# Other priority offsets in the table that breaks ties between operations of a fused attention and mixture-of-experts kernel

## The chip, the cores and the metric

The kernel runs on one core of a Trainium2 chip. Its time is device microseconds of one execution. Five engines work side by side: PE (TensorE, matrix multiplication), DVE (VectorE), ACT (ScalarE), POOL (GpSimd) and SP (SyncE, which here only starts transfers). Each takes its own list of instructions strictly in the order in which the list was written; an instruction whose inputs aren't there holds all that stands behind it on its engine.

## The reference

A decaying attention without softmax, of 8 batches and 8 heads with 576 tokens and 64 elements a head, and a layer of 8 experts on its result, of which each token uses two:

```python
scores = scale * np.matmul(q, k.transpose(0, 1, 3, 2))
gamma = 1.0 - 2.0 ** (-5.0 - np.arange(H))
Dmat = np.where(rel >= 0, gamma[:, None, None] ** rel[None, :, :], 0.0)
x = np.matmul(scores * Dmat, v)            # -> (4608, 512)
noisy = x @ w_gate + np.log1p(np.exp(x @ w_noise)) * noise
top2 = np.argpartition(-noisy, 2, axis=1)[:, :2]   # their softmax: top2_w
for e in range(8):
    for k in range(2):
        mask = top2[:, k] == e
        h = np.maximum(x[mask] @ w1[e], 0.0)       # 512 -> 1024
        out[mask] += top2_w[mask, k, None] * (h @ w2[e])
```

## The kernel before

**Attention** comes in 16 units of four heads of one batch; four units make a batch pair. SP loads q, k and v (L663 and L673). They are cast to bf16 and scaled with the decay: k on ACT (L712), q on DVE or POOL (L721), v on DVE or POOL (L728). PE turns k and q (L750, L744), and the copies out of PSUM go to ACT (L459) or DVE (L461). PE makes scores (L775), which DVE multiplies by the mask as it takes them out of PSUM (L783); then states (L808, into a tile `tb`) and outputs (L843, L853), which ACT or DVE copy into `xT`. The 64 last tokens of each batch pair are a tail of their own: casts L878 (ACT), L881 and L884 (DVE or POOL), turns L893, scores L908 and L913.

**The route** of each batch pair follows its tail: logits (L967), a chain of some 40 small DVE instructions (L977 to L1065) that finds the two experts of each token, ranks on PE (L1030, L1032) from a tile `MM` (L1003), a product `ub` on POOL (L1041), and a table: DVE makes two one-hot tiles, `olo` and `oh` (L1074), ACT writes the values `val` into the same PSUM tile (L1063), DVE multiplies (L1076), PE multiplies the two (L1081). From it come the row numbers `xi` (L1095). The rows of x are turned (L1110) and stored to `xd` in DRAM by SP.

**The experts** gather their rows from `xd` (L1246, indirect DMAs that POOL issues, two of them for one tile pair, with a small memset L444 between two that follow one another). What is filled from the first three batch pairs is computed already between the attention units (up L1328, down L1418), the rest afterwards in wide tiles (L1354, L1418, L1437; relu L1337 and L1339; scaling L1471, L1473; scatter L1483).

**What sets the order.** The program is recorded as operations with their inputs and outputs, and a planner writes the five lists out. It goes through the ready operations and takes the one that can start first by its own costs; of those that can start within the same twentieth of a microsecond, the one with the lowest priority:

```python
key = (round(t * 20), o.prio, o.i)
```

An operation that two engines may do goes to the one on which it ends first by the same costs. Every call site has a name, and a table `ORDER` of 149 names with six columns adds an offset to the priority. The column is chosen by how far on the operation lies: four of them for attention, one for the batch pair at its end and one for the wide tiles:

```python
prio += ORDER[at][min(3, int(max(0.0, prio)) // 4) if prio < 60 else 4 if prio < 136 else 5]
```

The choice of one operation moves all that come later, since tiles and PSUM buffers are handed out in the same pass. In the first 170 us of its plan the planner also puts matrix multiplications on PE that nothing reads (L467, the fillers), where it expects PE to wait for data.

Of the kernel before, what the change touches and what calls it, by code (L numbers as in the profile page):

```python
# [38 lines left out]
    "setup1": (-7.25, -7.25, -7.25, -7.25, -7.25, -7.25),  # L39
    "setup2": (5, 5, 5, 5, 5, 5),  # L40
    "setup3": (-4.25, -4.25, -4.25, -4.25, -4.25, -4.25),
    "setup4": (-0.25, -0.25, -0.25, -0.25, -0.25, -0.25),
    "setup5": (-3.25, -3.25, -3.25, -3.25, -3.25, -3.25),
    "setup6": (-1.75, -1.75, -1.75, -1.75, -1.75, -1.75),
    "setup7": (2, 2, 2, 2, 2, 2),
    "setup8": (4, 4, 4, 4, 4, 4),
    "setup9": (-6.5, -6.5, -6.5, -6.5, -6.5, -6.5),
    "setup10": (2, 2, 2, 2, 2, 2),
    "setup11": (2.5, 2.5, 2.5, 2.5, 2.5, 2.5),
    "setup12": (-0.5, -0.5, -0.5, -0.5, -0.5, -0.5),  # L50
    "setup13": (3.5, 3.5, 3.5, 3.5, 3.5, 3.5),
    "setup14": (-6, -6, -6, -6, -6, -6),
    "setup15": (1, 1, 1, 1, 1, 1),
    "setup16": (4.25, 4.25, 4.25, 4.25, 4.25, 4.25),
    "setup17": (-2.5, -2.5, -2.5, -2.5, -2.5, -2.5),
    "setup18": (-1.75, -1.75, -1.75, -1.75, -1.75, -1.75),
    "setup19": (-0.25, -0.25, -0.25, -0.25, -0.25, -0.25),
    "setup20": (-4, -4, -4, -4, -4, -4),
    "setup21": (0.5, 0.5, 0.5, 0.5, 0.5, 0.5),
    "setup22": (1.5, 1.5, 1.5, 1.5, 1.5, 1.5),  # L60
    "setup23": (-0.25, -0.25, -0.25, -0.25, -0.25, -0.25),
    "setup24": (-2.5, -2.5, -2.5, -2.5, -2.5, -2.5),
    "setup25": (-0.5, -0.5, -0.5, -0.5, -0.5, -0.5),
    "setup26": (2.25, 2.25, 2.25, 2.25, 2.25, 2.25),
    "setup27": (1.75, 1.75, 1.75, 1.75, 1.75, 1.75),
    "setup28": (1, 1, 1, 1, 1, 1),
    "setup29": (-3.25, -3.25, -3.25, -3.25, -3.25, -3.25),
    "setup30": (-3.5, -3.5, -3.5, -3.5, -3.5, -3.5),
    "setup31": (-1.5, -1.5, -1.5, -1.5, -1.5, -1.5),
# [12 lines left out]
    "later4": (-1, -1, -1, -1, -1, -1),
    "later5": (0.25, 0.25, 0.25, 0.25, 0.25, 0.25),
    "later6": (5.5, 5.5, 5.5, 5.5, 5.5, 5.5),
    "later7": (7.25, 7.25, 7.25, 7.25, 7.25, 7.25),
    "load1": (1, -1, -2, -3, 1, 1),
    "load2": (-6.75, -4.25, -9.25, -7, -8, -8),
    "load_tail1": (-1.5, -3.5, -1.75, -5.5, -1.5, -1.5),
    "cast1": (0, 0, -0.5, 0, 0, 0),
    "cast2": (-2, 0, 0, 2.5, 0, 0),  # L90
    "cast3": (-1, 1, -5.25, -2, -1, -1),
    "tr1": (-0.5, 2, -1, -1, 0, 0),
    "tr2": (0, 0, 1, 0, 0, 0),
# [1655 lines left out]
```

## Time and profile before

| what | value |
|---|---|
| median of 3 runs | 421.04 us (415.92, 421.04, 424.44) |
| profiled execution | 412.69 us, its span 411.1 us |
| mean granted TensorE clock | 0.989 |
| PE, POOL, ACT, DVE busy | 92%, 71%, 66%, 36% of the span |
| matrix multiplications | 4320, of them 68 fillers |
| moved by DMA | 98.06 MB |

The profile is of one execution, whose time lies below all three timed ones. L numbers are lines of the kernel. The name behind "<-" in brackets is what ended the idle time of an engine; "issue" there means that nothing in the profile did. All times within the span count from its start.

### The profile page before, as it was taken

How to read it: one execution, taken by the hardware profiler on the slowest of the kernel's cores; microseconds unless marked ns; L12 is line 12 of the kernel's file. 1: busy time of each engine (PE TensorE's matmuls, PEld its weight loads, DVE VectorE, ACT ScalarE, POOL GpSimd, SP SyncE). 2: the span in 40 equal slices, each digit the busy share in tenths (PEclk: the TensorE clock that was granted, in tenths of full speed). 3: DMA queues.
4: the chain of work that ended last, by engine and by line, in shares of the span. 5: the costliest groups of instructions: out<-in, count | busy, mean ns of one | idle time of the engine just before them, and what ended most of it. 6: DMA issues, size and time to landing. Idle time of an engine off the chain costs nothing.

```text
span 411.1 us, 11031 instructions
## 1 busy us (share of the span) xinstructions
PE 377.1 (92%) x4320; PEld 233.3 (57%) x4320; DVE 148.2 (36%) x413; ACT 272.3 (66%) x468; POOL 291.0 (71%) x379
## 2 busy tenths in 40 slices
PE   4998867889898898999999999999999999999994
PEld 2567656677575666767556554544554454454453
DVE  8456798788269587220111322101011000000002
ACT  2589978898787765776555877666686445555451
POOL 8676783990799848778676477778675776728564
PEclk9899999989999999999999999999999999999999
DMA  8999998999999989999989899999999998839766
GB/s 226 290 298 255 317 305 254 306 269 252 275 286 205 264 188 284 395 246 221 280 188 377 288 331 223 260 251 230 296 257 211 165 202 152 164 45 133 127 94 131
DMA packets 106184, 98.06 MB, mean 239 GB/s; under 512 B 40975, under 2 KB 83472, under 8 KB 106130
## 3 DMA queue, kind: packets, MB, share of 16 engines
q1 hardware_dynamic: 85858, 60.92, 56.0%
q0 software_dynamic: 17584, 36.24, 43.4%
q8 instruction: 34, 0.56, 0.6%
q10 hardware_dynamic: 2688, 0.18, 0.4%
q14 instruction: 20, 0.16, 0.2%
HBM read 73.11 MB, written 26.10 MB: 241 GB/s over the span
## 4 chain that ended last, share of the span: by engine, by line
PE 65%; DVE 8%; POOL 7%; DMA 6%; issue 6%; ACT 6%; POOLq 0%; SPq 0%; another core or an unknown queue 0%; DVEq 0%; ACTq 0%
PE ps L1418 25%; PE ps L1354 23%; PE ps L1328 6%; POOL out_dram L1483 4%; DMA xd<-xg 2%; ACT half L459 2%; DMA half<-in_v_dram 2%; DVE half L783 2%; PE ps L1437 2%; PE ps L808 2%; PE ps L467 1%; POOL half L721 1%; ACT xT L459 1%; DVE olo L1074 1%; PE ps L1268 1%
## 5 line engine op out<-in xcount | busy, mean ns | idle before, releaser
L1337 ACT ACTIVATE half<-ps 128x512 bf16<-128x512 f32 (+5 forms) x184 | 90.6, 503 | 87.5 <-PE ps L1354 55.0
L1418 PE MATMUL ps<-W,half 128*128 128x512 bf16 x432 | 137.8, 379 | 1.4 <-issue 1.1
L1354 PE MATMUL ps<-big,W 128*128 128x512 bf16 (+4 forms) x448 | 124.5, 326 | 0.6 <-DVE half L1473 0.6
L1246 POOL DMA_INDIRECT xg<-xd,xi x76 | 79.1, 1040 | 48.2 <-DMA half<-in_v_dram 11.7
L1483 POOL DMA_INDIRECT out_dram<-half,xg x71 | 90.3, 1272 | 30.1 <-issue 14.8
L1418 PEld LDWEIGHTS <-half 128*128 128x128 bf16 x568 | 54.5, 98 | 62.8 <-issue 3.1
L1354 PEld LDWEIGHTS <-W 128*128 128x128 bf16 x448 | 43.8, 98 | 33.4 <-issue 0.8
L1354 PE MATMUL ps<-big,xT 128*128 128x512 bf16 (+2 forms) x160 | 47.6, 337 | 0.0
L1471 ACT ACTIVATE half<-ps,xg 128x512 f32<-128x512 f32 (+1 forms) x58 | 39.3, 678 | 10.0 <-PE ps L1418 6.7
L783 DVE TENSOR_TENSOR half<-ps,mask 128x512 bf16<-128x512 f32 x64 | 40.3, 682 | 14.3 <-PE ps L775 10.9
L1418 PE MATMUL ps<-xT,half 128*128 128x512 bf16 x136 | 44.9, 379 | 0.0
L459 ACT ACTIVATE half<-ps 128x1024 bf16<-128x1024 bf16 (+1 forms) x42 | 38.5, 946 | 7.9 <-PE ps L744 4.0
L1473 DVE TENSOR_SCALAR half<-ps,xg 128x512 f32<-128x512 f32 (+1 forms) x17 | 10.6, 623 | 76.8 <-PE ps L1437 42.0
L1328 PE MATMUL ps<-half,W 128*128 128x256 bf16 (+1 forms) x288 | 29.1, 255 | 1.6 <-DVE half L461 0.8
L1339 DVE TENSOR_SCALAR half<-ps 128x512 bf16<-128x512 f32 (+5 forms) x12 | 6.8, 569 | 60.5 <-issue 32.9
L1328 PEld LDWEIGHTS <-W 128*128 128x128 bf16 x288 | 23.7, 98 | 5.8 <-issue 1.8
L467 PE MATMUL ps<-mask,ident__61 128*128 128x512 bf16 x68 | 20.3, 429 | 3.7 <-DVE hpf L527 3.7
L1469 DVE SCALAR_TENSOR_TENSOR half<-ps,xg,half 64x256 f32<-64x256 f32 (+2 forms) x7 | 3.6, 521 | 55.2 <-PE ps L1437 32.4
L1354 PEld LDWEIGHTS <-xT 128*128 128x128 bf16 x160 | 15.6, 98 | 12.8 <-issue 0.4
L459 ACT ACTIVATE tb<-ps 64x512 bf16<-64x512 f32 x32 | 18.9, 591 | 4.0 <-POOL half L721 1.9
L459 ACT ACTIVATE W<-big 128x1024 bf16<-128x1024 f32 x20 | 21.0, 1059 | 0.0
L808 PE MATMUL ps<-half,half 64*64 64x64 bf16 (+2 forms) x512 | 17.2, 213 | 1.7 <-ACT xT L459 1.6
(204 smaller groups left out, 517.0 us busy)
## 6 DMA issues: line engine op xcount, KB each, us to landing
big<-in_moe_w_dram SPq DMA_DIRECT2D x40, 512.0 KB
W<-in_moe_w_dram POOLq DMA_DIRECT2D x12, 512.0 KB
xd<-xg SPq DMA_DIRECT2D x16, 264.0 KB
W<-in_q_dram SPq DMA_DIRECT2D x16, 256.0 KB
big<-in_k_dram SPq DMA_DIRECT2D x8, 512.0 KB
big<-in_v_dram SPq DMA_DIRECT2D x8, 512.0 KB
big<-in_q_dram SPq DMA_DIRECT2D x16, 256.0 KB
W<-in_k_dram SPq DMA_DIRECT2D x6, 512.0 KB
```

Source lines behind the costliest of these rows:

```text
L459: self.nc.scalar.activation(out, in_, Act.Copy)
L467: self.nc.tensor.matmul(b.t, lhsT=ident, rhs=mask.rearrange("p r x -> p (r x)").unsqueeze(1).to_broadcast([P, 2, 2 * P]), start=True, stop ...
L783: nc.vector.tensor_tensor(S.t.bitcast(BF16).rearrange("p (h c x) -> p h c x", h=2, c=2)[:, h], p[h].t.rearrange("p (c x) -> p c x", c=2), ...
L808: nc.tensor.matmul(o[h * HD:(h + 1) * HD, hp, n, :], lhsT=kk[:k, r, c, y], rhs=vv[:k, r, c, y].unsqueeze(1).to_broadcast([k, n.stop - n.st ...
L1246: ins = nc.gpsimd.indirect_dma_start(out=x.t[:n, :], out_offset=None, in_=self.xd[:rows, :], in_offset=IOff(ap=xi.t[:n, h:h + 1], axis=0), ...
L1328: nc.tensor.matmul(pv()[:, f2, :], lhsT=w.t[:, o:o + P], rhs=xv()[:, di, :n], start=(di == 0), stop=(di == KD - 1))
L1337: self.nc.scalar.activation(o, i, Act.Relu)
L1354: self.mm = nc.tensor.matmul(p.t[:, :n], lhsT=w.t[:, o:o + P], rhs=xv()[:, di, :n], start=(di == 0), stop=(di == KD - 1))
L1418: self.mm = self.nc.tensor.matmul(po.t, lhsT=hv[:, c:c + P], rhs=self.W[e].t[:, o:o + DM], start=(f == 0), stop=(f == KF - 1))
L1471: nc.scalar.activation(y.t[q, c], x, Act.Copy, scale=g()[q])
L1473: nc.vector.tensor_scalar(y.t[q, c], x, g()[q], None, Alu.mult)
L1483: ins = nc.gpsimd.indirect_dma_start(out=self.out[:, :], out_offset=IOff(ap=ix()[q2], axis=0), in_=y.t[q2, :], in_offset=None, bounds_chec ...
```

## The change

All rows of the table are replaced; nothing else differs. Two of the rows, for `val` (L1063) and for the q casts (L721):

```diff
 ORDER = {
...
-    "cast2": (-2, 0, 0, 2.5, 0, 0),
+    "cast2": (14.75, 4, 13, -4, -1, -1),
...
-    "route35": (-3, -3, -4, -2.5, -3, -3),
+    "route35": (-7.5, -12.5, -11.25, -1.75, -7.5, -7.5),
...
 }
```

The order of SP's loads stays nearly the same, as do the wide tiles after some 200 us and the last instructions. The number of instructions on PE is the same, with 68 fillers again. Between engines these moved: L461 on DVE from 23 to 33 (L459 on ACT from 164 to 154), five of these ten lie between the one-hot tiles of the second and the fourth route; L721 on DVE from 2 to 4 (on POOL from 14 to 12), both new ones between the second and the third, L881 on DVE from none to 1 (on POOL from 4 to 3), small memsets of the setup (L597) on DVE from 7 to 29. The places that matter below follow.

ACT in the route of the third batch pair, where `val` (L1063) is written. Before:

```order
L459 ACTIVATE half1_83<-ps1_125 128x1024
L459 ACTIVATE half20_102<-ps2_126 128x1024
L1063 ACTIVATE ps3_127<-vals_160 128x18
L459 ACTIVATE xT_108<-ps4_128 128x2x16x16
L459 ACTIVATE xT_108<-ps5_129 128x2x16x16
L1471 ACTIVATE half0_82<-ps0_124,xg6_115 128x512
```

and after:

```order
L459 ACTIVATE half12_94<-ps1_125 128x1024
L1471 ACTIVATE half10_92<-ps0_124,xg6_115 128x512
L459 ACTIVATE xT_108<-ps6_130 128x2x16x16
L459 ACTIVATE xT_108<-ps2_126 128x2x16x16
L1063 ACTIVATE ps3_127<-vals_160 128x18
L459 ACTIVATE tb2_105<-ps6_130 64x8x64 x2
```

The two copies into `xT` stood behind `val` and now stand ahead of it.

DVE in the same route, where the first one-hot tile (`olo`) is made. Before:

```order
L1057 TENSOR_SCALAR ps_127<-ps_127 128x18
L1058 CAST ps_127<-ps_127 128x18
L1060 TENSOR_SCALAR ps_127<-ps_127 128x18
L1061 SCALAR_TENSOR_TENSOR ps_127<-ps_127,hi 128x18
L1065 COPY keep_t<-ps_127 128x2x9
L1074 TENSOR_TENSOR olo<-iota,ps_127 128x2304
L783 TENSOR_TENSOR half_94<-ps_125,mask 128x512
L783 TENSOR_TENSOR half_94<-ps_126,mask 128x512
```

and after:

```order
L1057 TENSOR_SCALAR ps_127<-ps_127 128x18
L783 TENSOR_TENSOR half_97<-ps_129,mask 128x512
L783 TENSOR_TENSOR half_97<-ps_128,mask 128x512
L783 TENSOR_TENSOR half_82<-ps_125,mask 128x512
L783 TENSOR_TENSOR half_82<-ps_124,mask 128x512
L1058 CAST ps_127<-ps_127 128x18
L1060 TENSOR_SCALAR ps_127<-ps_127 128x18
L1059 TENSOR_SCALAR hi<-ps_127 128x18
L1061 SCALAR_TENSOR_TENSOR ps_127<-ps_127,hi 128x18
L1074 TENSOR_TENSOR olo<-iota,ps_127 128x2304
```

The four score evictions stood behind `olo` (two of them are shown) and now stand ahead of it; `val` waited for `olo` and now waits for L1057.

POOL where the rows of the second batch pair are gathered first and the casts of the third pair's last units stand. Before:

```order
L1246 DMA xg_115<-xd,xi_186 128x264
L444 MEMSET idle 128x256
L1246 DMA xg_115<-xd,xi_186 128x264
L881 TENSOR_TENSOR half_82<-half_83,tabt 128x2x4x64
L1246 DMA xg_116<-xd,xi_186 128x264
L884 TENSOR_TENSOR half_91<-half_99,tab 128x512
L721 TENSOR_TENSOR half_96<-big_80,tabq 128x2x8x64
L728 TENSOR_TENSOR half_89<-big_81,tab 128x4x2x64
```

and after:

```order
L1246 DMA xg_115<-xd,xi_186 128x264
L444 MEMSET idle 128x256
L1246 DMA xg_115<-xd,xi_186 128x264
L444 MEMSET idle 128x256
L1246 DMA xg_116<-xd,xi_186 128x264
L884 TENSOR_TENSOR half_87<-half_98,tab 128x512
L1246 DMA xg_116<-xd,xi_186 128x264
L728 TENSOR_TENSOR half_96<-big_81,tab 128x4x2x64
```

The tail's cast L881 and the q cast L721 of this place are now on DVE, next to one another; as many gathers as before stand ahead of the tail's L884, and one more ahead of the v casts.

ACT in the first microseconds, at the first k casts (L712) and the exponentials of the decay tables (L515, L518, L536). Before:

```order
L515 ACTIVATE tab<-tab 128x40
L518 ACTIVATE tabq<-tabq 128x32
L536 ACTIVATE tabt<-tabt 128x8
L627 DMA noise<-in_moe_noise_dram 64x4x32
L712 ACTIVATE half_83<-W_122 128x4x2x64 x2
```

and after:

```order
L515 ACTIVATE tab<-tab 128x40
L631 DMA noise<-in_moe_noise_dram 64x4x8
L627 DMA noise<-in_moe_noise_dram 64x4x32
L712 ACTIVATE half_83<-W_122 128x4x2x64
L518 ACTIVATE tabq<-tabq 128x32
L712 ACTIVATE half_83<-W_122 128x4x2x64
```

The exponential of `tabq` now stands between the two k casts. On DVE the five small instructions that make its input (L502 to L505 and L516) now stand behind the cast of the gate weights (L617), which they preceded. On PE 12 fillers stand ahead of the first turn of k and 8 behind it, where 11 and 10 stood.

## Rows read from the trace of the kernel before

**Rows 1.** The page: busy time of PE, and the chain that ended last.
```profile
PE 377.1 (92%) x4320; PEld 233.3 (57%) x4320; DVE 148.2 (36%) x413; ACT 272.3 (66%) x468; POOL 291.0 (71%) x379
PE 65%; DVE 8%; POOL 7%; DMA 6%; issue 6%; ACT 6%; POOLq 0%; SPq 0%; another core or an unknown queue 0%; DVEq 0%; ACTq 0%
```

**Rows 2.** Stretches: length, busy time of each engine, granted clock, DMA share, GB/s.
```profile
0.00:10.00 10.00, 4.50 (x18) 1.91 (x19) 8.12 (x64) 3.00 (x6) 8.26 (x54) 0.99 0.87 223
10.00:50.00 40.00, 35.97 (x804) 25.94 (x802) 24.07 (x51) 32.46 (x51) 28.17 (x62) 0.96 1.06 290
50.00:100.00 50.00, 39.81 (x1032) 32.93 (x1029) 43.92 (x110) 42.00 (x69) 34.20 (x40) 0.97 1.05 278
100.00:120.00 20.00, 17.70 (x346) 12.94 (x344) 7.73 (x18) 15.78 (x28) 14.14 (x13) 1.00 1.10 290
120.00:150.00 30.00, 25.88 (x503) 19.37 (x501) 23.37 (x77) 23.46 (x44) 22.93 (x32) 1.00 1.09 236
150.00:200.00 50.00, 48.16 (x428) 33.05 (x426) 16.19 (x42) 31.18 (x53) 41.02 (x65) 1.00 1.00 271
200.00:400.00 200.00, 199.35 (x1157) 103.34 (x1156) 22.10 (x54) 122.79 (x218) 137.03 (x114) 1.00 0.99 212
```

**Rows 3.** Stretches of PE alone: its busy time, granted clock, DMA share, GB/s.
```profile
10.00:13.00 3.00, 3.00 (x11) 0.50 1.15 306
81.00:85.00 4.00, 2.12 (x52) 0.98 1.11 313
85.00:88.00 3.00, 3.00 (x53) 0.50 1.09 243
```

**Rows 4.** What PE waited for: total us, times, longest.
```profile
PE ps L750 <- ACT xT L459: 2.5, 1, 2.5
PE ps L893 <- POOL half L881: 1.6, 1, 1.6
PE ps L775 <- DVE pay L1012: 1.1, 1, 1.1
PE ps L775 <- ACT xT L459: 1.1, 2, 0.8
```

**Rows 5.** Timeline of ACT at the routes: start, us, instruction, idle time before.
```profile
60.80 0.19 ACT L1063 ACTIVATE ps<-vals 128x18 f32<-128x18 f32 x1 [2.19 <-DVE olo L1074]
60.93 1.13 ACT L712 ACTIVATE half<-W 128x512 bf16<-128x512 f32 x2
132.00 0.19 ACT L1063 ACTIVATE ps<-vals 128x18 f32<-128x18 f32 x1 [2.62 <-DVE olo L1074]
132.12 1.07 ACT L459 ACTIVATE xT<-ps 128x512 bf16<-128x512 f32 x2
```

**Rows 6.** Timeline of DVE in the third batch pair's route.
```profile
128.46 0.17 DVE L1057 TENSOR_SCALAR ps<-ps 128x18 int32<-128x18 int32 x1
131.88 1.28 DVE L783 TENSOR_TENSOR half<-ps,mask 128x512 bf16<-128x512 f32 x2
...
143.68 0.20 DVE L1095 TENSOR_TENSOR xi<-L,ps 128x40 int32<-128x40 f32 x1
```

**Rows 7.** Timeline of POOL: a gather, and the fourth route's product.
```profile
105.14 1.11 POOL L1246 DMA_INDIRECT xg<-xd,xi  x1 [11.66 <-DMA half<-in_v_dram]
...
148.65 0.45 POOL L1041 TENSOR_TENSOR ub<-MM,bnd 128x144 f32<-128x144 bf16 x1 [4.38 <-DVE keep_w L1006]
```

**Rows 8.** Groups by line and shape on DVE: busy, mean ns, idle before.
```profile
L461 DVE COPY half<-ps 128x1024 bf16<-128x1024 bf16 x5 | 3.4, 689 | 2.6 <-PE ps L1268 2.0 <-issue 0.3 <-remote 0.3
L721 DVE TENSOR_TENSOR half<-W,tabq 128x1024 bf16<-128x1024 f32 x2 | 2.4, 1218 | 0.0
```

**Rows 9.** Timeline of DVE in the first microseconds.
```profile
5.88 2.88 DVE L617 CAST wgn<-half 128x64 bf16<-128x64 f32 x1 [0.28 <-DMA half<-in_moe_w_noise_dram]
```

**Rows 10.** Timeline of ACT in the first microseconds.
```profile
8.95 0.61 ACT L712 ACTIVATE half<-W 128x512 bf16<-128x512 f32 x1
```

**Rows 11.** Timeline of PE in the first microseconds.
```profile
10.12 3.84 PE L467 MATMUL ps<-mask,ident__61 128*128 128x512 bf16 x10
```

More of the change, by code (lines that the diff above doesn't have):

```diff
@@ L49 @@
[L49 to L69, printed above, removed]
@@ L179 @@
[L179 to L187 removed]
+    "setup1": (-7.5, 11, 11, 11, 11, 11),
+    "setup2": (13.75, 1, 1, 1, 1, 1),
@@ new lines @@
+    "setup13": (5, -1, -1, -1, -1, -1),
+    "setup14": (-3.5, -9, -9, -9, -9, -9),
+    "setup15": (-11.5, -1.5, -1.5, -1.5, -1.5, -1.5),
+    "setup16": (-18.5, -2.75, -2.75, -2.75, -2.75, -2.75),
+    "setup17": (-4.5, -4, -4, -4, -4, -4),
+    "setup18": (-12.25, -13.5, -13.5, -13.5, -13.5, -13.5),
+    "setup19": (18.75, 7.5, 7.5, 7.5, 7.5, 7.5),
+    "setup20": (-5.5, -5.5, -5.5, -5.5, -5.5, -5.5),
+    "setup21": (-0.25, -7, -7, -7, -7, -7),
+    "setup22": (-1, 1.25, 1.25, 1.25, 1.25, 1.25),
@@ new lines @@
+    "setup33": (-20, -6.5, -6.5, -6.5, -6.5, -6.5),
+    "setup34": (-21.5, -12, -12, -12, -12, -12),
+    "setup35": (-10, -1, -1, -1, -1, -1),
+    "setup36": (9.25, 0.5, 0.5, 0.5, 0.5, 0.5),
+    "setup37": (15.75, 0, 0, 0, 0, 0),
+    "setup38": (15.25, -2.5, -2.5, -2.5, -2.5, -2.5),
+    "setup39": (10.25, 0.25, 0.25, 0.25, 0.25, 0.25),
+    "setup40": (12, -2.5, -2.5, -2.5, -2.5, -2.5),
+    "later1": (-16, -5, -5, -5, -5, -5),
+    "later2": (-9.5, -4.75, -4.75, -4.75, -4.75, -4.75),
+    "later3": (9.25, 2.25, 2.25, 2.25, 2.25, 2.25),
@@ new lines @@
+    "tail2": (8.5, -11, 3.25, 9.75, 5.75, 5.75),
+    "tail3": (6.5, -0.5, 3.25, 2, 1, 1),
+    "tail4": (-3.25, 9, 0.5, -15.5, 0.75, 0.75),
+    "tail5": (24.25, 5, 14.25, 7.75, 6, 6),
+    "tail6": (4.25, -3.5, -1.5, 2.25, -2.25, -2.25),
+    "tail7": (8.25, 8.75, 10.5, 21.25, 8, 8),
+    "tail8": (-7.75, 8.75, -0.5, -5.25, -0.25, -0.25),
+    "tail9": (19, -2.75, 6.75, 5, 2.75, 2.75),
+    "route1": (1.5, -9.25, 19.25, 17, 8, 8),
+    "route2": (-2.25, -5.75, 25.75, -10.25, -2.25, -2.25),
+    "route3": (-12, -17.75, -6.25, -4, -12, -12),
@@ new lines @@
+    "fetch8": (-2, -2, -2, -2, -3.5, 4.75),
+    "mix1": (-2.5, -2.5, -2.5, -2.5, 12.25, -2.5),
+    "mix2": (18.25, 18.25, 18.25, 18.25, 16, 18.25),
+    "mix3": (1.25, 1.25, 1.25, 1.25, -6, 1.25),
+    "up1": (6, 6, 6, 6, -7.75, 13.75),
+    "wide1": (5, 5, 5, 5, 5, -0.25),
+    "wide2": (3.25, 3.25, 3.25, 3.25, 3.25, -1.25),
+    "finish1": (1.75, 1.75, 1.75, 1.75, 1.75, -5.25),
+    "finish2": (2.75, 2.75, 2.75, 2.75, -7.25, 5.25),
+    "finish3": (11.5, 11.5, 11.5, 11.5, 30.75, 5.5),
+    "finish4": (9.25, 9.25, 9.25, 9.25, 9.25, 3.25),
@@ L188 @@
+    "record1": (7.5, 7.5, 7.5, 7.5, -1, 17.25),
+    "record2": (0.75, 0.75, 0.75, 0.75, 0.75, 12.75),
+    "record3": (1.25, 1.25, 1.25, 1.25, 1.25, -2.25),
+    "record4": (8.5, 8.5, 8.5, 8.5, 8.5, 23.25),
 }
```

224 lines of the change are left out of this document (98 added, 126 removed).

## The prediction

> **What bounds the kernel now.** The page says that PE is busy for 92% of the span and that the chain which ended last runs 65% on PE [rows 1]: PE's idle time is what a new order can win. The table of stretches says where that idle time lies [rows 2]. From 200 to 400 us PE is busy for 199.35 of 200, so the wide tiles can't be shortened by their order; 11.10 of the span lies behind them, and the order of their end is the old one. Before 200 PE stands idle for 5.5 us in 0 to 10, 4.0 in 10 to 50, 10.2 in 50 to 100, 2.3 in 100 to 120, 4.1 in 120 to 150 and 1.8 in 150 to 200, together 28. To that comes the granted clock: it is 0.50, the lower of its two levels (1.2 GHz), from 10 to 13 and from 85 to 88, the second time after a stretch of 4 us in which PE had worked for only 2.12 [rows 3]. Three microseconds at half speed do 1.5 of work, so each cold stretch costs about 1.5. All that the table of offsets can win lies in these 31 us, and the new order has to be read at the waits that make them: the list of PE's waits gives the largest [rows 4].
>
> **The change, wait by wait.** Times are those of the profiled execution, 412.69 us, which stands 8.35 below the median of the runs. I work out a difference and put it on the median, 421.04.
>
> *Start.* The cast of the gate weights (L617) took 2.88 us for 64 columns and ended at 8.76 [rows 9]; the five instructions that make the input of `tabq` now stand behind it, and one for the tail's table beside them. Six in a row at 0.17 each, the duration of a small one like L1057 [rows 6], are 1.0; with about 0.2 for the exponential (I take it like the small write L1063, 0.19 [rows 5]) the second k cast, which stands behind that exponential on ACT, can start at about 10.1 instead of 8.95 [rows 10]: 1.2 later with the gaps between them. The turn of k waits for it. Behind the turn stood ten fillers in 3.84 us, 0.38 each [rows 11]; now there are eight, 0.77 less. So the first turn of q, and with it the first scores, come 0.4 later. The q cast, also behind `tabq`, moves to 10.2 and ends, at 1.22 [rows 8], by 11.4, under the fillers that reach to 14; without these it would cost that 1.2 itself. Bounds: −0.8 (L617 isn't held this time, and only the fillers go) and +1.2 (they don't help). I take +0.4.
>
> *First route.* ACT stood still for 2.19 us ahead of L1063, until DVE's `olo` was done, and the two k casts and the `xT` copies queued behind it; PE's turn of the next k waited 2.46 for such a copy, the 2.5 of the list [rows 4, 5]. The new order keeps L1063 behind `olo` but puts one of the two casts ahead of it: half of 1.13, 0.57, earlier for the copy, less one small DVE instruction put ahead of `olo`, 0.2. Bounds 0 and −0.6; I take −0.4.
>
> *Tail of the second pair.* PE's turn L893 waited 1.6 us for the cast L881 on POOL [rows 4], which stood behind two gathers, the first of which had held POOL for 11.66 until 105.14 [rows 7]. L881 is on DVE now, and DVE has 12.3 of 20 us free from 100 to 120 [rows 2], so this wait goes. What is late next is L884 and the v casts on POOL: two casts have left the list ahead of the v casts, and one gather of 1.11 [rows 7] has come in; so they are not later than now. Bounds 0 (PE meets the next wait) and −1.6; I take −1.6, because no other of PE's large waits lies in this place.
>
> One row speaks against that. L617, on DVE, was drawn out to 2.88 us while POOL cleared tiles [rows 9], so casts on DVE and work on POOL may hold each other. The Trainium skill, "GPSIMD Engine Reference", section "1. Specifications", states that GpSimd shares its SBUF interfaces with VectorE, and that it contends with instructions there that have two SBUF inputs; the moved casts have two. By that rule the moved L881 and L721 would hold POOL's L884 for as long as they take, 1.9 us, and the sum below would have +0.3 in place of −1.6: −0.8 instead of −2.7. The q casts on DVE that took 1.22 [rows 8] were not drawn out, and by that row I leave the −1.6; the other case is part of the last rival.
>
> *Third route.* ACT stood for 2.62 ahead of L1063, which waited for `olo`; two `xT` copies were behind it [rows 5], and PE's scores waited for these, twice, 1.1 in all [rows 4]. Now the copies precede L1063, which waits only for L1057, done at 128.6 [rows 6], so the wait goes: −1.1. DVE does four score evictions first, two of which took 1.28 [rows 6]: `olo` comes 2.6 later, and so does the table that ends in `xi` at 143.88 [rows 6], now 146.5. Two gathers with that `xi` now stand ahead of L1041 on POOL; at 1.11 each [rows 7] they are through at 148.7, and L1041 started at 148.65, after POOL had stood idle for 4.38 [rows 7]. What hid this is that idle time, and it is used up: if the gathers also wait for the stores of the third pair's rows, the whole fourth route waits with them, and I put 0 to +2.2 on it and take 0, since the stores do not depend on `olo`.
>
> *Second route.* PE waited 1.1 for the payload [rows 4] between two halves of scores. One half and the ranks change places, and the same payload now stands ahead of the states: 0, with −1.1 and +0.8 as bounds (the wait itself; half of a cold stretch more).
>
> The ten copies that move from ACT to DVE take 0.69 each there [rows 8] and free ACT, which no wait above names beyond those counted: 0. **Sum**: 0.4 − 0.4 − 1.6 − 1.1 = −2.7. That is 410.0 for the profiled execution and **418.3** on the median.
>
> **The rivals.**
>
> *The order wins far more.* The waits named are the longest, but the new order moves hundreds of instructions from 50 to 150, where PE is idle for 16.6 us. If it takes away all 6.4 of 100 to 150 and half of the 10.2 of 50 to 100, the cold stretch at 85 included, that is −11.5: 409.5. For it: early expert work, which waits for nothing but weights and gathers, lies further forward in PE's list, so that it can fill such holes. Against it: PE keeps the same 68 fillers, so the planner still expects the same holes.
>
> *The order doesn't decide.* The DMA share of the table stands at 1.05 to 1.10 from 10 to 150, higher than in the wide tiles behind [rows 2], and SP's loads come in the same sequence: what is won in front of one load is lost waiting for the next one. The waits move and the time stays, 421.0, with 2 either way for the waits' own scatter. Against it: the list of PE's waits names engines, not transfers. By the Trainium skill, "DMA: Bandwidth & Descriptors", section "Issuing engines are not separate DMA queues", transfers of all engines interleave on the same 16 DMA engines, so POOL's gathers, moved forward, would come out of the same share as the loads; this trace agrees as far as its shares go.
>
> *DVE becomes the bound, and it is slower.* Place: 105 to 150, the third and fourth route. DVE gets two q casts of 1.22, one tail cast (priced as a copy, 0.69) and five of the ten copies, 3.4: 6.6 us more [rows 8], which is all of the 6.6 that it has free of 30 from 120 to 150 [rows 2]. From the point where its free time is used up, every score eviction (L783) comes late, and PE waits for it one for one. If the 12.3 free from 100 to 120 take none of it, the gains above are lost, and it is +6.6 and +0.4 at the start. The three moved casts, 3.1 us, may be drawn out beside POOL as L617 was [rows 9], which I put at their own length once more. Together +10.1: 431.1. Against it: the q casts stand where DVE has time, and copies lie between evictions where DVE waits for PE.
>
> **How the numbers follow.** My forecast has 0.40, its own range, from the bounds, 416 to 422. The large gain has 0.26 (405 to 413), the order that doesn't decide 0.14 (419 to 423), DVE as the bound 0.20 (426 to 436). The range that leaves out the far ends of the second and the last (0.07 and 0.12) is 407 to 430. A measurement of this kernel, whose three runs lie 2% apart, can tell a change of about 2%, 8.4 us: faster is below 412.6, which holds nearly all of the large gain and a little of the forecast, 0.29; slower is above 429.5, three quarters of the last rival, 0.15; within lies 0.56.
>
> **What would show it.** Right: L1063 of the third route starts near 129 behind two `xT` copies and PE has no wait for `xT` there; L893 waits for nothing on POOL; the second k cast starts near 10.2 and the first turn of q at 14.2; PE's idle time from 100 to 150 falls from 6.4 to under 4; the cold stretches stay. The large gain would show as idle time under 5 from 50 to 100 and a granted clock of 1.00 from 85 to 88. That the order doesn't decide would show as PE's waits naming transfers, with the same idle time. DVE as the bound would show as DVE busy for over 28 of the 30 us from 120 to 150, and PE waiting for L783. I am wrong on the fourth route if L1041 starts later than 149 with a gather ahead of it that waits for a store.

## The result, and the profile after

| | before | after |
|---|---|---|
| median of 20 runs each | 415.06 us (411.89 to 424.44) | 419.32 us (416.65 to 423.49) |
| profiled execution, its span | 412.69, 411.1 us | 417.45, 415.7 us |
| mean granted clock in it | 0.989 | 0.981 |

The ratio is 1.0113, 95% interval [1.0085, 1.0141]: the kernel became 1.1% slower on that chip, where 0.65% faster (418.3 on 421.04) was forecast. The sign is wrong. That 419.32 lies near the 418.3 is luck: the forecast stood on the median of three runs, 421.04, and the median of 20 of the same kernel is 415.06. Ratios here leave disturbed, slower runs out, and three of the profiles read below (of e1, the second h run and c3) are of such runs and weigh less.

The page of after, its first row, the chain that ended last, and the DMA queue that carries instructions (packets, MB, share of 16 engines):

```profile
PE 378.0 (91%) x4320; PEld 236.1 (57%) x4320; DVE 158.8 (38%) x445; ACT 262.4 (63%) x459; POOL 290.4 (70%) x355
q8 instruction: 34, 0.56, 0.5%
PE 70%; DVE 10%; issue 7%; ACT 6%; POOL 5%; DMA 1%; another core or an unknown queue 0%; ACTq 0%; POOLq 0%; DVEq 0%
```

PE does the same work in the same time [rows 1]; what is added is idle time. The stretches of after, columns as in [rows 2]:

```profile
0.00:10.00 10.00, 5.17 (x17) 1.88 (x18) 6.62 (x56) 3.02 (x6) 8.24 (x35) 1.00 0.87 217
10.00:50.00 40.00, 34.22 (x807) 25.68 (x806) 25.08 (x77) 31.91 (x51) 29.07 (x59) 1.00 1.08 288
50.00:100.00 50.00, 38.56 (x949) 32.21 (x948) 42.26 (x107) 38.38 (x64) 34.62 (x41) 0.90 1.04 277
100.00:120.00 20.00, 17.26 (x338) 12.21 (x336) 11.14 (x18) 14.51 (x26) 13.47 (x14) 1.00 1.14 297
120.00:150.00 30.00, 26.60 (x553) 21.00 (x545) 25.44 (x66) 21.15 (x40) 18.87 (x26) 1.00 0.89 193
150.00:200.00 50.00, 46.84 (x422) 32.72 (x423) 23.31 (x66) 29.77 (x51) 35.26 (x56) 0.97 0.98 271
200.00:400.00 200.00, 199.19 (x1172) 103.88 (x1171) 22.27 (x55) 119.59 (x217) 142.50 (x121) 1.00 0.94 217
```

The wide tiles are as full as before. Idle time of PE up to 200 is 31.4 in place of 28.0, longer by 1.75 from 10 to 50 (where before, at the half clock, took 1.5 more for its work), by 1.25 from 50 to 100 and by 1.3 from 150 to 200, the last two with a lower granted clock than before. When the same piece of PE's work starts in the two traces (worked out from the start times):

```
start of                      before    after    after - before
first scores (L775)            15.52    13.63     -1.9
the 129th matmul of L775       36.87    36.83      0.0
the 257th                      66.64    68.34     +1.7
the 353rd                      90.04    94.55     +4.5
the 481st                     130.56   135.00     +4.4
first wide tile (L1354)       199.02   203.28     +4.3
last instruction's end        411.1    415.7      +4.5
```

So the startup gained, that gain was gone by 37, and the trace of after falls behind between 37 and 90. That alone doesn't place the loss: three more executions of the changed kernel (c1, d1 and f1 below), which lose nothing in the median, reach the 353rd at 94.1 to 95.0 as well, and yet the first wide tile at 196.6 to 198.1, ahead of the 199.0 of before. What PE waited for up to 205 in after (total us, times, longest; the rows left out between these name engines); "issue" is a wait that nothing in the profile ends:

```profile
PE ps L1110 <- issue: 3.9, 3, 1.8
...
PE ps L750 <- ACT xT L459: 2.7, 1, 2.7
PE ps L1030 <- DVE MM L1003: 2.2, 2, 1.6
PE ps L843 <- issue: 1.9, 3, 0.9
PE ps L893 <- DVE half L881: 1.7, 1, 1.7
...
PE ps L908 <- issue: 1.5, 1, 1.5
...
PE ps L1418 <- ACT half L1337: 1.1, 1, 1.1
```

Three of these have no cause in the profile. With the smaller ones, the waits on "issue" come to 9.0 us here and to 3.9 in the first profile of before, whose two largest stand first below; a second profile of before (g1, below; 20 to 200) has 2.8, of which the rows behind them are the largest:

```profile
PE ps L843 <- issue: 2.4, 5, 1.2
PE ps L1418 <- issue: 1.1, 1, 1.1
...
PE ps L843 <- issue: 1.4, 1, 1.4
PE ps L744 <- issue: 0.7, 1, 0.7
PE ps L1328 <- issue: 0.5, 1, 0.5
```

**What these pauses are.** The timeline of PE in after at two of them (start, us, instruction, idle before):

```profile
97.86 0.61 PE L1110 MATMUL ps<-ident__61,xT 128*128 128x128 bf16 x8
99.02 0.62 PE L1110 MATMUL ps<-ident__61,xT 128*128 128x128 bf16 x8 [0.55 <-issue]
...
148.66 0.65 PE L1110 MATMUL ps<-ident__61,xT 128*128 128x128 bf16 x5
150.88 1.35 PE L1110 MATMUL ps<-ident__61,xT 128*128 128x128 bf16 x11 [1.57 <-issue]
```

PE stops in the middle of 16 matmuls of one line with the same operands. Counting the recorded PE instructions (weight loads and matmuls, in order of start), the long pauses begin at number 961, 1217, 2497, 3009, 3521 and 5313: each is 193 plus a multiple of 256. The queue q8 moves 34 packets in all, 0.56 MB or 16.5 KB each, and PE's 8,690 recorded instructions fill 34 blocks of 256. In the trace one such packet starts a mean of 3.3 us after PE has passed such a number (1.2 to 6.0, up to 135; a mean of 2.6 in the trace of before), takes about 1.1 us, and PE goes on 1.3 to 1.6 us after it has landed. At the pause of 84.21 to 86.25 the packet lay from 83.5 to 84.6; PE, and the one packet of q8 between 83 and 85:

```profile
83.86 0.56 PE L1110 MATMUL ps<-ident__61,xT 128*128 128x128 bf16 x7
86.25 0.44 PE L1110 MATMUL ps<-ident__61,xT 128*128 128x128 bf16 x5 [1.83 <-issue]
q8 instruction: 1, 0.02, 3.5%
```

Over all 20 profiles there are 87 such pauses of more than 0.5 us up to 200, and each ends 1.2 to 1.8 us after the landing of a packet of q8: PE waits for its next block. So where PE runs through a block of 256 in less than some 5.8 us (3.3, 1.1 and 1.4), as it does in attention and in the routes, it mostly stands still at the block's end, but not always: it came to number 4289 in 4.9 us without a pause, as that packet had started 1.7 us after the boundary before. Why a packet starts early or late is not shown. The Trainium skill, "Runtime: NRT & Kernel Launch", section "Instruction fetch mechanics", states the block of 256 instructions and the queue, and that the cost of passing a boundary is "mostly hidden"; the blocks agree with this trace, the cost does not: up to 2.0 us each here. I call the sum of these pauses after 50 us the *late pauses*: those over 0.3 us, from the start of the last instruction before to the start of the next, where no engine or transfer ends the wait. They are 2.3 us before, 6.9 after; a pause just at the limit counts or not by a few hundredths, so a sum is good to some 0.4. Not every wait on "issue" is one: the 1.1 of before at L1418 lies at no such number.

### The profile page after: what moved, and what is told of

Same layout as the page of the kernel before. It is cut to its first block, busy times and chain, and to the rows that moved or that the text cites. A ratio compares the mean times of both kernels' runs of the same rounds, so it can differ in the third digit from the quotient of the medians.

```text
span 415.7 us, 11016 instructions
## 1 busy us (share of the span) xinstructions
PE 378.0 (91%) x4320; PEld 236.1 (57%) x4320; DVE 158.8 (38%) x445; ACT 262.4 (63%) x459; POOL 290.4 (70%) x355
## 4 chain that ended last, share of the span: by engine, by line
PE 70%; DVE 10%; issue 7%; ACT 6%; POOL 5%; DMA 1%; another core or an unknown queue 0%; ACTq 0%; POOLq 0%; DVEq 0%
PE ps L1418 25%; PE ps L1354 21%; PE ps L1328 7%; POOL out_dram L1483 4%; ACT half L459 2%; DVE half L783 2%; PE ps L1110 2%; PE ps L808 2%; PE ps L843 2%; PE ps L775 2%; PE ps L1437 1%; PE ps L750 1%; PE ps L1268 1%; PE ps L744 1%; DMA half<-in_moe_w_noise_dram 1%
## 5 line engine op out<-in xcount | busy, mean ns | idle before, releaser
L1337 ACT ACTIVATE half<-ps 128x512 bf16<-128x512 f32 (+5 forms) x183 | 89.8, 505 | 82.3 <-PE ps L1354 50.7
L1418 PE MATMUL ps<-W,half 128*128 128x512 bf16 x432 | 138.5, 381 | 0.0
L1246 POOL DMA_INDIRECT xg<-xd,xi x76 | 81.6, 1073 | 45.6 <-issue 11.7
L1418 PEld LDWEIGHTS <-half 128*128 128x128 bf16 x568 | 54.7, 98 | 62.4 <-issue 3.1
L1471 ACT ACTIVATE half<-ps,xg 128x512 f32<-128x512 f32 x60 | 41.3, 688 | 17.0 <-PE ps L1418 8.2
L1473 DVE TENSOR_SCALAR half<-ps,xg 64x256 f32<-64x256 f32 (+1 forms) x15 | 8.6, 572 | 102.3 <-PE ps L1437 59.8
L1418 PE MATMUL ps<-xT,half 128*128 128x512 bf16 x136 | 45.2, 379 | 1.4 <-ACT half L1337 1.1
L459 ACT ACTIVATE half<-ps 128x1024 bf16<-128x1024 bf16 (+1 forms) x38 | 34.9, 946 | 11.9 <-PE ps L744 7.6
L459 ACT ACTIVATE tb<-ps 64x512 bf16<-64x512 f32 x32 | 18.9, 589 | 7.1 <-PE ps L808 4.9
L467 PE MATMUL ps<-mask,ident__61 128*128 128x512 bf16 x68 | 18.9, 414 | 3.5 <-POOL ident__61 L539 3.5
L459 ACT ACTIVATE xT<-ps 128x512 bf16<-128x512 f32 (+1 forms) x35 | 17.7, 551 | 5.6 <-PE ps L1268 2.4
L728 POOL TENSOR_TENSOR half<-big,tab 128x512 bf16<-128x512 f32 x16 | 16.6, 1054 | 2.0 <-DMA big<-in_v_dram 1.9
L728 POOL TENSOR_TENSOR half<-W,tab 128x512 bf16<-128x512 f32 x16 | 16.9, 1065 | 1.4 <-DMA W<-in_v_dram 1.3
```

What stands on the lines that cost most here:

```text
L459: self.nc.scalar.activation(out, in_, Act.Copy)
L467: self.nc.tensor.matmul(b.t, lhsT=ident, rhs=mask.rearrange("p r x -> p (r x)").unsqueeze(1).to_broadcast([P, 2, 2 * P]), start=True, stop ...
L728: self.eng(e).tensor_tensor(o, i, t, Alu.mult)
L1246: ins = nc.gpsimd.indirect_dma_start(out=x.t[:n, :], out_offset=None, in_=self.xd[:rows, :], in_offset=IOff(ap=xi.t[:n, h:h + 1], axis=0), ...
L1337: self.nc.scalar.activation(o, i, Act.Relu)
L1418: self.mm = self.nc.tensor.matmul(po.t, lhsT=hv[:, c:c + P], rhs=self.W[e].t[:, o:o + DM], start=(f == 0), stop=(f == KF - 1))
```

## The experiments

Ratios are to the kernel before on the same chip. The groups ran on chips of different speed (median of before 419.45 for the e and h runs, which shared a chip; 411.25 for c; 411.73 for d; 411.22 for f; 411.32 for g), so runs are compared within a letter. Which chip the result ran on is not recorded; its median of before, 415.06, is like none of these, so I take it for another one. "Control" is the changed kernel unedited.

| run | what | ratio [95%] | late pauses, us |
|---|---|---|---|
| e1 | after, L1063 first | 0.9967 [0.9928, 1.0006] | 3.7 |
| e2 | after, 11 fillers | 1.0008 [0.9966, 1.0050] | 2.6 |
| h first | before, two new columns | 1.0072 [1.0029, 1.0116] | 3.0 |
| h second | before, four new columns | 1.0101 [1.0057, 1.0145] | 2.6 |
| c1 | control | 1.0006 [0.9973, 1.0039] | 6.7 |
| c2 | after + 24 PE instructions | 0.9921 [0.9891, 0.9952] | 2.4 |
| c3 | after + 102 | 0.9953 [0.9919, 0.9986] | 2.1 |
| c4 | before, L1063 first | 0.9951 [0.9919, 0.9984] | 2.5 |
| d1 | control | 1.0021 [0.9988, 1.0054] | 5.5 |
| d2 | after, L881 earlier | 1.0000 [0.9969, 1.0031] | 6.9 |
| d3 | e1 + d2 + 24 | 0.9933 [0.9893, 0.9973] | 1.1 |
| d4 | before + 24 | 0.9925 [0.9888, 0.9962] | 5.3 |
| f1 | control | 0.9971 [0.9934, 1.0007] | 6.5 |
| f2 | after + 24 | 0.9912 [0.9882, 0.9943] | 0.9 |
| f3 | after + 256 | 1.0027 [0.9993, 1.0060] | 7.7 |
| f4 | after + 280 | 0.9946 [0.9911, 0.9981] | 3.2 |
| g1 | before, one execution | | 2.8 |
| g2 | c4 + 24 | 0.9955 [0.9921, 0.9989] | 2.2 |

**First route, e1 and e2.** In e1 the changed kernel records the values before the one-hot tile; in e2 that wait stays, and PE gets 11 fillers ahead of the states (L808) of that place.

```diff
 # e1: one operation put elsewhere in the planned order
+    x = at("route35", 0); order.remove(x); order.insert(order.index(at("route30", 0)) + 1, x)
 # e2
+    at("states1", 7)[0].fill = 22
```

> The changed kernel with one instruction recorded elsewhere: in the first route, val (L1063, ACT) is recorded right behind L1057 and so ahead of olo, and needn't wait for it. Theory A (the first route costs the time: PE stands still for 2.71 us until 62.94, and from 62.6 to 69.4 its granted clock is 0.50): the wait of ACT (2.45 us) and that of PE go, the clock stays at 1.00 there, and the time falls by 2.5 to 5 us, to a ratio of 0.999 to 1.005 to the kernel before. Theory B (the loads pace attention, so what is won here is lost at the next load): wait and cold clock go, the ratio stays at 1.010 to 1.012. Theory C (the loss sits behind 80 us): as B, but the scores of unit 9 start earlier by 2 us than in the changed kernel and the lead is lost only behind 80.

> The changed kernel with 11 filler matrix multiplications more, ahead of the states (L808) of unit 7, so that PE is busy through the 2.71 us in which the first route holds it; the wait of ACT for olo stays. If the half clock behind the stall is what costs (theory A, its second half), the granted clock stays at 1.00 from 62 to 69, worth up to 3.4 us, ratio 1.002 to 1.006. If the stall itself costs, or the loads pace everything (theory B), the clock is mended and the ratio stays at 1.009 to 1.013.

In e1 PE's wait at L750 fell from 2.7 to 0.2, and in both the granted clock was 1.00 from 62 to 69 (0.51 in after). Ratios of 0.9967 and 1.0008 stand below the 1.0113 of the result, and below what every theory gave them, but no control ran on that chip, and the controls elsewhere make this comparison worthless: inconclusive by itself. The 11 fillers of e2 are also 22 PE instructions more, so e2 is nearly the shift by 24 of the next runs.

**Half of the table, h.** The kernel before with the new values in its first two columns alone, or in its last four alone.

```diff
-    "route35": (-3, -3, -4, -2.5, -3, -3),
+    "route35": (-7.5, -12.5, -4, -2.5, -3, -3),
 # and so for every row; the other run takes the other four columns
```

> The kernel before with the new values in the first two columns of the table only (units 0 to 7, the setup and the first route), the old in the other four. If the loss lies in the setup and the first route (theory A), the ratio is 1.005 to 1.012, and the first route shows the stall and the cold clock of the changed kernel. If it lies behind (theory C), it is 0.995 to 1.003: the start is 1.9 us earlier, and the loads take that back.

> The kernel before with the new values in the last four columns only (units 8 to 15, the last three routes, the experts), the old in the first two. If the loss lies in the first route (theory A), the ratio is 0.995 to 1.004. If it lies behind 80 us (theory C: the second route and the tail casts on DVE), it is 1.007 to 1.013, with the waits of PE at L1110 and L843 near 86 and 92 and at L893 near 114.

Each half alone was slower, 1.0072 and 1.0101, and both profiles show few late pauses. By the ratios the first fits theory A and the second theory C, which exclude each other, and in the first PE doesn't wait at L750 behind the first route, but 2.5 at L775 for another copy. What they lose may lie in the mix of old and new orders, which nothing here shows; these two don't place the loss.

**The blocks, c1 to c3.** The shift cuts fillers at the start into four of a quarter of the width: 6 PE instructions more each, the same columns.

```diff
-        for _ in range(n // 2):
-            self.nc.tensor.matmul(b.t, lhsT=ident, rhs=<mask, 512 wide>, ...)
+        for o, i in fillers(b.t, whole, mask, n // 2):      # the first 4 (c3: 17) yield four pieces of 128
+            self.nc.tensor.matmul(o, lhsT=ident, rhs=i, ...)
```

> The changed kernel once more, unedited, as the control beside the next two. Every theory: ratio 1.005 to 1.016 to the kernel before, and the gaps without a wait (over 0.7 us, in the middle of a run of matmuls) at the same PE instructions as in its first trace, the 961st, 1217th, 2497th, 3009th and 5313th recorded, 0.9 to 2.0 us each, some 7 to 9 us in all.

> The changed kernel with 4 of the fillers ahead of the first projection each cut into 4 of a quarter of the width: 24 PE instructions more (12 matmuls, 12 weight loads), the same columns, nothing else moved. Theory F (TensorE's instructions come in blocks of 256, and where it runs through a block faster than the next arrives it stands still): the gaps stay at the recorded instructions 193 + 256 k, so at work that lies 24 instructions earlier in the program; in the runs of attention and of the routes this meets the same dense stretches, so the sum of the gaps stays at 7 to 10 us and the ratio at 1.005 to 1.016. Rival A (the loss is the wait of the first route, 2.71 us, and the half clock behind it): nothing there changes, ratio 1.005 to 1.016. Rival N (the gaps belong to certain pieces of work, not to a count): the gaps stay at the same matmuls of the program, at recorded numbers higher by 24.

> The same with 17 fillers cut: 102 PE instructions more, the same columns. Theory F: the gaps stay at the recorded instructions 193 + 256 k, which are now pieces of work 102 instructions earlier, and by the times of the trace of after more of the blocks then end in slow stretches: the sum of the gaps falls from about 9 to some 4 to 6 us, and the ratio to 0.997 to 1.006. Rival A (first route's wait and the half clock behind it): those stay at 2.7 us and about 7 us, ratio 1.005 to 1.016. Rival N: gaps at the same matmuls of the program, numbers higher by 102, sum and ratio unchanged.

The control stood at 1.0006, where every theory gave 1.005 to 1.016: the 1.1% of the result is not there on this chip. Its long pauses lay again at 193 + 256 k (2753, 4289, 5057 and 5313, the last three read up to 6 lower where records are missing), but not at the same ones: 2497 and 3009, 1.7 and 2.0 us in after, have none. So the count says where a pause can lie, and the execution which of them come and how long. Rival N falls: in c2 the pause at 2753 is no longer in L967 but in L775, 24 instructions earlier in the program. Rival A can't make c2's gain: PE's wait at L750 was 2.7 there and 2.8 in c3, as in the control. But theory F had the sizes wrong: I forecast no gain for c2, and it was the larger of the two, 0.9915 of the control; c3 gained a little more than forecast (0.997 to 1.006).

**Was it the cutting? f1 to f4.** A shift by a whole block must bring the boundaries back to the same work; 280 must act as 24. "Control" in the next texts is f1.

> The changed kernel unedited, a fourth time, as the control of this call; the three after it are compared with it. Ratio to the kernel before 0.998 to 1.014, as it has been; gaps without a wait of 7 to 9 us in all at the recorded instructions 193 + 256 k (a few numbers lower late in the program, where records are missing).

> The changed kernel with 24 PE instructions more at the start, as in the earlier run, on this call's chip. Theory F (the place of the block boundaries in the program sets the gaps): 0.990 to 0.995 of the control, gaps of 2 to 4 us in all. If the earlier gain was that chip's alone: 0.997 to 1.003 of the control.

> The changed kernel with 256 PE instructions more, one whole block: 42 fillers, nearly all of them before 30 us, each cut into 4, and one into 3; the same columns. Theory F: from 30 us on the boundaries lie at the same work as in the control, so the same gaps (7 to 9 us in all, at the same matmuls of the program) and 0.997 to 1.003 of the control, although ten times as many instructions were added as in the run ahead of this. Rival S (what gains is the cutting of the fillers itself, by the clock or the start): at least as fast as the run with 24, 0.985 to 0.995 of the control.

> The changed kernel with 280 PE instructions more, one block and 24. Theory F: as the kernel with 24, 0.990 to 0.995 of the control, gaps of 2 to 4 us. Rival S: as the kernel with 256, whatever that is.

f2 and f3 differ in how many fillers are cut, 4 and 43, and the one with more gains nothing: 0.9912 against 1.0027, with f4 at 0.9946 between. Rival S falls for the changed kernel. f4 is 0.9919 of f3, as theory F has it, but 0.9975 of the control f1, where 0.990 to 0.995 was forecast. The timeline of PE in f3 at the two places shown above of after:

```profile
99.73 0.61 PE L1110 MATMUL ps<-ident__61,xT 128*128 128x128 bf16 x8
100.95 0.62 PE L1110 MATMUL ps<-ident__61,xT 128*128 128x128 bf16 x8 [0.61 <-issue]
...
145.89 0.65 PE L1110 MATMUL ps<-ident__61,xT 128*128 128x128 bf16 x5
148.55 1.26 PE L1110 MATMUL ps<-ident__61,xT 128*128 128x128 bf16 x15 [2.00 <-issue]
```

The pauses are between the same matmuls, 8 of 16 and 5 of 16, with numbers 3777 and 5569 instead of 3521 and 5313: 256 more. In f2 the whole of 50 to 200 has one wait on "issue" (first row), where f1, the control, has these among its largest (rows behind it):

```profile
PE ps L853 <- issue: 0.4, 1, 0.4
...
PE ps L967 <- issue: 2.2, 1, 2.2
PE ps L1110 <- issue: 1.1, 1, 1.1
```

Over the four, the time follows the late pauses in order: 0.9, 3.2, 6.5 and 7.7 us, and 0.9912, 0.9946, 0.9971 and 1.0027. From the least to the most that is 6.8 us of pauses and 1.15% or 4.7 us of time, some 0.7 for one, an estimate from one profile of each. f4 has 5.5 us of pauses before 50, f2 none; but by the same 0.7 the difference of their late pauses, 2.3, is 1.6 us already, and their times differ by 1.4. So what is lost that early seems to come back, as it would where loads pace that part. f3 was forecast within 0.3% of its control and lies 0.56% above it; more of its pauses are early ones too, and I leave that rest open.

**The tail, d1 and d2.**

```diff
 # d2: DVE's L881 of the second pair's tail ahead of the copy that waits for PE
+    x = at("tail2", 2); order.remove(x); order.insert(order.index(at("out_3", 23)) + 1, x)
```

> The changed kernel unedited, a third time, beside the next three. So far the same program has stood at 1.0113 and, on another chip, at 1.0006 of the kernel before. If the loss belongs to the order itself, the ratio is 1.008 to 1.014; if it belongs to where the blocks of instructions happen to arrive, and with that to the chip and the run, it may lie anywhere from 0.998 to 1.014. In the profile: L881 on DVE at about 110 takes 0.7 us (PE's wait at L893 0.3) or, where L728 runs on POOL beside it, 1.8 to 2.1 us (wait 1.4 to 1.7).

> The changed kernel with DVE's L881 of the second pair's tail recorded ahead of the copy of turned rows (L461) that waits for PE. Theory P (it lost the 1.6 us that the prediction gave it because it stood behind that copy and so met POOL's L728): L881 starts right behind the cast of L461, 1.5 to 2 us earlier, takes 0.68 to 0.75 us, PE's wait at L893 is under 0.4 us, and the ratio to the unedited kernel of this call is 0.996 to 1.000. Rival (late loads of the tail pace it): L881 starts no earlier than 110 and holds the copy behind it; ratio to the unedited kernel 1.000 to 1.004.

The control is at 1.0021, d2 at 1.0000; the intervals overlap. Theory P held in the trace: L881 started at 108.78, took 0.68, and PE no longer waited at L893. What decides its length is what POOL does beside it. DVE first, POOL behind it, in after:

```profile
111.43 0.69 DVE L461 COPY xg<-ps 128x1024 bf16<-128x1024 bf16 x1 [1.28 <-PE ps L1110]
112.04 2.11 DVE L881 TENSOR_TENSOR half<-half,tabt 128x512 bf16<-128x512 f32 x1
114.08 1.21 DVE L721 TENSOR_TENSOR half<-big,tabq 128x1024 bf16<-128x1024 f32 x1
...
111.53 2.07 POOL L728 TENSOR_TENSOR half<-big,tab 128x512 bf16<-128x512 f32 x2
```

and in f1, the same program on another chip:

```profile
109.68 0.68 DVE L881 TENSOR_TENSOR half<-half,tabt 128x512 bf16<-128x512 f32 x1
110.28 3.44 DVE L721 TENSOR_TENSOR half<-big,tabq 128x1024 bf16<-128x1024 f32 x1
...
109.51 1.03 POOL L1246 DMA_INDIRECT xg<-xd,xi  x1 [0.17 <-issue]
110.56 2.06 POOL L728 TENSOR_TENSOR half<-big,tab 128x512 bf16<-128x512 f32 x2
```

A DVE cast beside POOL's gather keeps its 0.68; beside POOL's casts it takes about its own time and what is left of theirs: 0.68 becomes 2.11, and 1.21 becomes 3.44 beside two of them (f1). In d1 one POOL cast of 1.08 (L884) made 1.75 of it. It goes the other way too: at 10.77 in after POOL's L728 took 1.33, at 10.47 in c1 1.70, in place of 1.04, while DVE's L721 beside it kept 1.22. Which of the two DVE casts of the tail is hit depends on a few tenths of a us. The Trainium skill, "GPSIMD Engine Reference", section "1. Specifications", states that GpSimd shares its SBUF interfaces with VectorE and contends there with DVE instructions that have two SBUF inputs; these traces agree. PE's wait at L893 was 1.7 in after and 1.3 in d1, where L881 was drawn out, and 0.3 in c1 and f1, where it wasn't. As d1 and c1 have about the same ratio, that alone isn't what made the 1.1%.

**Versions that might beat both, c4, d3, d4, g2.** c4 and g2 move L1063 of the first and third route in the kernel before, as e1 does in the first; d3 and d4 are sums of edits shown above.

> The kernel before with L1063 of the first and of the third route recorded right behind L1057, ahead of the copies of olo; nothing else moved. Rival A: PE's wait of 2.46 at L750 behind the first route goes to under 0.5, and the third route's wait for the turned rows too, ratio 0.985 to 0.995. Theory F alone: the waits go as well, but what was waited is handed on in part to the next late loads and blocks, ratio 0.992 to 1.000.

> The changed kernel with three edits: L1063 of the first route recorded right behind L1057, L881 as in the kernel ahead of this, and 24 PE instructions more at the start. If the three are worth what they showed apart (first route's wait of 2.7 us and the half clock behind it, the tail's 1.4, the blocks' 3 to 5 us), the ratio is 0.983 to 0.993 to the kernel before. If the gain of the shift was that of one program and one chip, it is 0.993 to 1.003.

> The kernel before with the same 24 PE instructions more at the start, nothing else moved. Theory F: its blocks end in other stretches too, but by the times of its trace the sum of the gaps hardly changes (3.5 us in its profile, 3.0 to 3.8 by its times at the shift): ratio 0.996 to 1.004. Rival S (the cut fillers themselves are worth something, by the clock or the time of the start): the ratio falls as it did with the changed kernel, to 0.990 to 0.994.

> The kernel before with L1063 of the first and third route recorded right behind L1057 and 24 PE instructions more at the start, the two edits that apart stood at 0.9951 and 0.9925. If they touch different waits, 0.984 to 0.991; if both only move the boundaries of the blocks to better places, no better than one of them, 0.991 to 0.998.

> The kernel before unedited, for a second profile of it. If the loss of the first result lay in more and longer gaps at the blocks' boundaries, the kernel before has fewer of them in any execution: 3 to 5 us in all against 7.8 to 8.9 us in the four profiles of the changed kernel. If the two are alike there, 7 to 9 us here too.

All four beat the kernel before, by 0.45 to 0.75%, none by 2%. c4's 0.9951 lies at the edge of rival A and within theory F alone, and the edits don't add up: d3, at the edge of its sum, does no better than 24 instructions alone, g2 no better than c4. d4 went as rival S said, 0.9925 where 0.996 to 1.004 was expected, and its one profile shows 5.3 us of late pauses, more than the kernel before, from an execution of 410.68, 2.3 above its median. For the kernel before it thus stays open what 24 instructions change. With 24 more in both kernels, on two chips, they stand alike: 0.9921 (c2) and 0.9925 (d4). g1 confirmed the other half: 2.8 us of late pauses in a second execution of before, against 5.5 to 6.9 in four of after.

## Why the prediction was wrong, step by step

*What bounds the kernel*: right as far as it went. PE is the bound, the wide tiles did not move, the loss lies before 200. But of PE's idle time I read only the waits that name an engine; "issue", 6% of the chain in [rows 1], I read as nothing.

*Start, +0.4*: wrong. First scores came 1.9 earlier. ACT and PE in after:

```profile
9.17 0.61 ACT L712 ACTIVATE half<-W 128x512 bf16<-128x512 f32 x1
10.19 1.89 PE L467 MATMUL ps<-mask,ident__61 128*128 128x512 bf16 x8
```

The second k cast (9.17) came 0.2 later than before, not 1.2, since L617 took 2.12 instead of the 2.88 of [rows 9]; and the eight fillers ran at full clock in 1.89, where ten had taken 3.84 at half [rows 3, 11]. The second profile of before has a granted clock of 1.00 from 10 to 14 as well, so that cold stretch belonged to one execution and not to the order. None of it lasted: POOL's third q cast waited for its load and started at 40.96 against 40.82, which is the rival that loads pace, in the part up to 50.

*First route, −0.4*: wrong in sign. ACT's wait ahead of L1063 is longer than in [rows 5], and PE's behind it 2.7 instead of 2.5, after which the clock fell. ACT, and stretches of PE with clock, DMA share and GB/s, both of after:

```profile
58.59 0.63 ACT L712 ACTIVATE half<-W 128x512 bf16<-128x512 f32 x1
61.67 0.19 ACT L1063 ACTIVATE ps<-vals 128x18 f32<-128x18 f32 x1 [2.45 <-DVE olo L1074]
```

```profile
62.50:69.00 6.50, 6.06 (x98) 0.50 0.80 217
76.00:79.50 3.50, 3.33 (x84) 0.54 0.96 286
151.00:154.00 3.00, 3.00 (x38) 0.50 1.12 233
```

PE's 6.06 us of work at 1.2 GHz would take 3.0 at 2.4, so this stretch costs some 3.0, an estimate. In four executions of the changed kernel the clock from 62 to 69 was between 0.51 and 0.76, in two of the kernel before 1.00, behind a wait 0.1 to 0.6 shorter; e1 and d3, without the wait, had 1.00. But d4, the kernel before with 24 instructions more, waited 2.8 there and had 0.76, so this stretch is not the new order's alone. I had no term here for a stretch that turns cold. The other two cold stretches follow block pauses, that of number 2497 (72.6 to 74.3) and that of 5313 (149.1 to 150.9).

*Second route, 0*: no wait on the payload decides there; between 66.6 and 90 after loses 2.8 more, and in that stretch lie three block pauses, 1.7, 0.6 and 2.0, where before has one of 0.4. But c1, d1 and f1 come as late to the 353rd and end level with before, so this is not shown to reach the end.

*Tail, −1.6*: failed in the profile of the result, by the shared interfaces that I had weighed and set aside on the ground of casts that ran beside no cast of POOL, and the other way round: POOL's L728 drew out L881 itself. PE still waits 1.7. In the control c1 and f1 it came out as forecast but for 0.3.

*Third route, −1.1*: the wait for the turned rows is gone, as said, though L1063 stands at 135.9 and not near 129, as L1057 came at 135.6; but PE meets the next one:

```profile
127.93 0.24 PE L1030 MATMUL ps<-MM,ltri 128*128 128x144 bf16 x1 [1.60 <-DVE MM L1003]
```

*Fourth route, 0*: the sign that I named for being wrong came. POOL, in after:

```profile
149.64 1.07 POOL L1246 DMA_INDIRECT xg<-xd,xi  x1 [2.76 <-DMA xd<-xg]
...
159.93 0.45 POOL L1041 TENSOR_TENSOR ub<-MM,bnd 128x144 f32<-128x144 bf16 x1 [0.24 <-DVE keep_w L1006]
```

The gather waited for a store, and L1041 came at 159.9 instead of 148.65 [rows 7]. But POOL then stood idle for 6.3 until DVE's payload, so the gather isn't what held the route. In c1, d1 and f1 L1041 stands at 154.6 to 156.4, without a loss, so a later fourth route is not by itself the 1.1%. Of the rivals, DVE as the bound didn't come: it was busy for 25.4 of the 30 us from 120 to 150, where that rival needed 28.

*The sum, −2.7*: the step that failed is that each wait taken away was counted as time won, with PE's path between the named waits taken as unchanged. At the tail and in the third route PE met a wait of the same size (1.7 and 1.6) where −1.6 and −1.1 stood, and PE's idle time from 100 to 150 was 6.1, where I had forecast under 4. Two terms were put at nothing: pauses at every 256th instruction, 6.9 against 2.3 us after 50, and stretches that turn cold (half of one stood in a bound alone). Shown by the shifts is that the pauses exist, that their places move with the count of instructions, and that 24 instructions are worth 0.6 to 0.9% in the changed kernel (c2, f2), 102 some 0.5% (c3), and that a whole block gains nothing (f3). If some 0.7 of each reach the end, as in the f runs, the 4.6 more of them in after are +3.2; that is an estimate, and that they make the difference between the two kernels is not shown: the kernel before gains as much from the same edit (d4), with more late pauses in its profile. The clock is no better a candidate: its mean in the profile is 0.981 against 0.989, which is 3.3 us of 411, but c1's profile has 0.975 and its kernel stands at 1.0006. So the −2.7 is not there with the shift in both kernels (0.9921 and 0.9925) nor without it (1.0006, 1.0021, 0.9971), and on those chips the rival that the order doesn't decide, to which I gave 0.14, comes nearest; that loads are what paces is seen at the start alone.

*What stays open*: the changed kernel lost 1.1% on the chip of the result and nothing on three others (1.0006, 1.0021, 0.9971), with late pauses of like size. Against the control c1, the trace of after loses its 5.2 us up to the wide tiles behind 100 us: 2.6 by 116 (the drawn-out L881 and three short pauses at L843, L853 and L750 that lie at no block boundary), 1.8 at L1030, and 1.7 at 197 to 199, where L1418 waits for ACT's L1337; a pause that c1 alone has at 4289 takes off 1.0. The cold stretch from 151 adds nothing: the same work stands 3.5 apart ahead of it and 3.6 behind. Whether that chip makes these waits regularly was not tried; runs can't be placed on a chip at will. So the 1.1% is a result of that chip or of those runs, its cause stays open, and the order by itself is shown neither slower nor faster.

## What to carry to other kernels

Read the waits that name nothing: when a dense engine stops in the middle of a run of like instructions, number its instructions, and see whether the stops have a period. Where they do, a reorder of work, or a few instructions more or less far ahead, can move all of them at once, so a change of about 1% needs a control that shifts the count alone, and the unchanged program on a second chip, before it is put down to the order. And price a moved instruction by what will run beside it on the engine with which it contends, here DVE beside POOL, not by how long it took alone.

## What the runs showed of the hardware that was not expected

PE stops at recorded instruction 193 + 256 k for up to 2.9 us (d2, 76.43 to 79.29) when the packet of the next block comes late, mostly where it has run through a block in under some 5.8 us; it goes on 1.2 to 1.8 us after that packet has landed (87 pauses in 20 profiles). Two programs of equal work, 24 PE instructions apart, differ by 0.6 and 0.9% (f, c). DVE's cast L881, with two inputs in SBUF, takes 0.68 beside a gather of POOL, 1.75 beside one POOL cast (d1) and 2.11 beside two (after). And the same two programs differed by 1.1% on one chip and by 0.3% or less on three.
